# Two transformer-like layers on one core: the squares of two blocks folded to 64 columns before the norm matmuls, and one set of additions moved one tile earlier

## The chip, the cores and the metric

The kernel runs on one core of one Trainium2 chip. The metric is device time in microseconds (us) of the whole launch. The engines are TensorE (PE; its weight loads are shown apart as PEld), VectorE (DVE), ScalarE (ACT), GpSimd (POOL) and SyncE (SP, which here only starts DMAs).

## What is computed

Two attention layers and two gated layers, in turn, on 2048 tokens of 448 features. This is the reference, cut to its core:

```
def _A_ref(x, wqkv, wo):
    qkv = (x @ wqkv).reshape(B, S, 3, H, Dh), heads in front
    scores = einsum("bhqd,bhkd->bhqk", q, k) * (Dh ** -0.5)
    o = einsum("bhqk,bhkd->bhqd", softmax(scores), v)
    return o @ wo
def _B_ref(x, w_gate, w_up, w_down):
    return (sigmoid(x @ w_gate) * (x @ w_up)) @ w_down
x = A_x
x = x + _A_ref(_layernorm(x), A_wqkv, A_wo)
x = x + _B_ref(_layernorm(x), B_w_gate, B_w_up, B_w_down)
x = x + _A_ref(_layernorm(x), A_wqkv, A_wo)
x = x + _B_ref(_layernorm(x), B_w_gate, B_w_up, B_w_down)
```

## The kernel before

The tokens are worked on in four blocks of 512 (`NB` = 4, `W` = 512). Every fp32 operand is split into a high and a low fp16 part, so that a product is the sum of several fp16 matmuls. A layer has four stages: `project` (queries, keys, values), `attend`, `out_project`, and `gated`.

The change lies in `project` of the first layer, and there in `qk` (L834), which makes queries and keys of one block as seven tiles of 128 features by 512 tokens. For a tile:

- PE does 11 matmuls of 512 columns into one of four PSUM banks (L649).
- ACT copies the high part out of the bank (L883), DVE takes the low part (L884), and ACT squares the high part into `sq`, bf16, 128x512 (L886).
- DVE folds `sq`: it takes the larger of the first and the second half of its columns (L890), so that 256 are left. The loop there has two widths, 256 and 128, and stops at `few`, which is 256.
- SP starts the DMA of the tile to DRAM (L893).
- `norm_products` (L843) is put into the list `late`. It multiplies the folded `sq` by a table `ind` that sums over the features of each head, into PSUM (L845 for queries, L848 for keys). The largest such sum of a head bounds its scores, and keeps the exponentials in range: since the maximum over tokens is all that is wanted, folding by maximum only makes the bound a little looser.

`late` holds three tiles back: the norm matmul of tile i stands in PE's order behind the products of tile i+3. The last three tiles of a block are popped by `finish` (L899), which also reduces the 256 columns to one on DVE (L904, for queries and for keys). `finish` of block 2 is called within block 3, behind the products of its tiles 1 and 2; `finish` of block 3 is called in `guard_of_norms`, behind the first tile of values of block 2 (`vals`, 11 matmuls of 448 columns).

Beside each tile runs a list of other steps, `fill`: `fill[i]` is issued behind tile i. In blocks 2 and 3 of the first layer these are the splitting of the next block's operand (`b3.ready`: ACT L234, L239 and DVE L235, L240) and six steps `Measure.add` (L1313). Each of these sums the squares of a part of the weights of the later stages on DVE (L1318, a pass over up to 1792 columns with an accumulator read behind it, and a copy, L1322); the last, for gate and up, has one pass on DVE and one on ACT (L1325). All is issued in program order on each engine; no scheduler moves it.

```
for n in (W // 2, P):
    if n >= few:
        nc.vector.tensor_tensor(sq[:, 0:n], sq[:, 0:n], sq[:, n:2 * n], op=ALU.max)
```

The second layer makes queries and keys in another way (`qk_sums`), and folds its squares in two steps, of 2x128 and 2x64 columns (L961); its norm matmuls have 64 columns (L923), and its reductions 128 (L1101).

Of the kernel before, what the change touches and what calls it, by code (L numbers as in the profile page):

```python
# [19 lines left out]
P = 128  # L20
# [8 lines left out]
W = TB * P  # L29
# [48 lines left out]
ALONE = 3  # L78
CHUNK = D * NF // 7
SUMS_AT = ((("w", 3), 74), (("u", 0), 122), (("u", 6), 236))  # L80

N_SLOTS = 19
N_QUART = 12
# [44 lines left out]
def interleaved_layers(ctx: ExitStack, tc: tile.TileContext, x_in, wqkv, wo, w_gate, w_up,  # L128
# [31 lines left out]
    def bank(i, name):  # L160
        return psum(f"bank{i}", name, [P, 512])
# [479 lines left out]
    def by_features(pm, blk, wh, wl, some=range(11)):  # L641


        terms = [(w(kt), x[:, kt, :]) for kt in range(3)
                 for w, x in ((wh, blk.hi), (wh, blk.lo), (wl, blk.hi))]
        terms += [(w(3), blk.tail) for w in (wh, wl)]
        for i in some:
            w, x = terms[i]
            nc.tensor.matmul(pm, w, x, start=(i == 0), stop=(i == 10))  # L649
# [171 lines left out]
    def project(layer, wq, begun):  # L821
# [4 lines left out]
        def ones_of_values():  # L826
            for v in values:
                nc.gpsimd.memset(v[:, :, :, DH:VC], 0.0)
                nc.gpsimd.memset(v[:, :, :, DH:DH + 1], 1.0)
# [4 lines left out]
        def qk(b, blk, fill, before, ahead=()):  # L834
            pn = [bank(4 + 2 * (b % 2), "qnorm"), bank(5 + 2 * (b % 2), "knorm")]
            late = deque()
            few = W // 2

            def rows_of_heads(i):

                return ind[:, i:i + P // H, :].rearrange("p a h -> p (a h)")

            def norm_products(i, sq):  # L843
                if i <= 3:
                    nc.tensor.matmul(pn[0][:, 0:few], rows_of_heads(i), sq[:, 0:few],  # L845
                                     start=(i == 0), stop=(i == 3))
                if i >= 3:
                    nc.tensor.matmul(pn[1][:, 0:few], rows_of_heads(1 + i), sq[:, 0:few],  # L848
                                     start=(i == 3), stop=(i == 6))
                qrt.put(sq)  # L850

            def products(pm, i, some=range(11)):
                c = slice(i * P, (i + 1) * P)
                by_features(pm, blk, lambda kt: wq.qk[0][:, kt, c],
                            lambda kt: wq.qk[1][:, kt, c], some)

            begun = deque()
            if layer == 0 and b == 0:
                begun.extend(bank(i, "qkp") for i in range(2))
                for i, some in ((0, (0, 3, 1, 6, 2, 5, 8, 4)), (1, (0, 3, 6)), (0, (7,)),  # L860
                                (1, (1, 4, 7)), (0, (9, 10))):
                    products(begun[i], i, some)
            rest = {0: (), 1: (2, 5, 8, 9, 10), 4: (0, 3, 6, 1, 4, 7, 9, 2, 5, 8, 10)}

            for i in range(7):
                c = slice(i * P, (i + 1) * P)
                pm = begun.popleft() if begun else bank(evac[0] % 4, "qkp")
                evac[0] += 1
                if layer == 0 and b == 0:
                    products(pm, i, rest.get(i, range(11)))  # L870
                else:
                    products(pm, i)
                if layer == 0 and b == 0:
                    along[i]()
                if before and i in (1, 2):
                    before(i == 2)
                if len(late) == 3:
                    late.popleft()()
                hl = qrt.get("qkhl", [P, 2, W], F16)
                sq = qrt.get("sq", [P, W], BF16)  # L880
                if i < len(ahead) and ahead[i]:
                    ahead[i]()
                nc.scalar.activation(hl[:, 0, :], pm, AF.Copy, scale=PS)  # L883
                nc.vector.scalar_tensor_tensor(hl[:, 1, :], pm, PS, hl[:, 0, :], op0=ALU.mult,  # L884
                                               op1=ALU.subtract)
                nc.scalar.activation(sq, hl[:, 0, :], AF.Square)  # L886

                for n in (W // 2, P):
                    if n >= few:
                        nc.vector.tensor_tensor(sq[:, 0:n], sq[:, 0:n], sq[:, n:2 * n],  # L890
                                                op=ALU.max)
                n = slice(b * W, (b + 1) * W)
                nc.sync.dma_start(qk_scr[c, :, n], hl)  # L893
                qrt.put(hl)
                late.append(lambda i=i, sq=sq: norm_products(i, sq))
                if i < len(fill) and fill[i]:
                    fill[i]()

            def finish(whole=True):  # L899

                while len(late) > (0 if whole else 1):
                    late.popleft()()
                for i in range(2 if whole else 0):
                    nc.vector.tensor_reduce(peaks[:, i, b:b + 1], pn[i][0:H, 0:few], axis=AX.X,  # L904
                                            op=ALU.max)
            return finish
# [217 lines left out]
        def vals(b, blk, after, tiles=range(TB), at=None, begun=None, banks=None):  # L1124
            for j in tiles:
                if banks:
                    pv = bank(banks[j], "vp")
                else:
                    pv = begun or bank(evac[0] % 4 if at is None else at, "vp")
                    evac[0] += 1  # L1130
                values_product(pv, blk, j, range(2, 4) if begun else range(4))
                if j in after:
                    after[j]()
                v, pv = values[b][:, j, :, 0:DH], pv[:, 0:D].rearrange("p (h d) -> p h d", d=DH)
                if at is None:
                    nc.scalar.activation(v, pv, AF.Copy, scale=PS)
                else:
                    nc.vector.tensor_scalar(v, pv, PS, None, op0=ALU.mult)
            if tiles[-1] == TB - 1:
                blk.drop()  # L1140
# [22 lines left out]
        blks = begun + [Block(b, layer == 1, True) for b in range(len(begun), NB)]  # L1163
        idle = None
        sq = lambda b, *js: lambda: blks[b].squares(js)
        b1, b2, b3 = blks[1:]
# [22 lines left out]
        if layer == 0:  # L1189
            fin = qk(0, blks[0], fill, None, ahead)  # L1190
            vals(0, blks[0], along_values)
            fill = [b2.gather, b3.norm, sq(3, 0, 1), sq(3, 2, 3), idle,
                    lambda: b2.ready(0, 1), lambda: (b2.ready(2, 3), b3.store())]
            fin = qk(1, b1, fill, None)
            vals(1, b1, {0: b3.gather, 2: fin})
            add = tell.add
            fin = qk(2, b2, [idle, lambda: b3.ready(0, 1), lambda: b3.ready(2, 3), idle, add, add,
                             add], None)
            fin = qk(3, blks[3], [add, add, add], fin)
        else:  # L1200
            b2.clear()
            ones_of_values()
            b3.apart = True
            h2, h3, s3 = b2.half_steps(), b3.half_steps(), b3.squared()
            both = lambda *steps: lambda: [do() for do in steps]
            order = (3, 0, 1, 6)
            fin = qk_sums(0, blks[0], {0: b1.later + s3[0:1], 1: h2[0:1], 2: h2[1:2], 3: s3[1:2],
                                       4: h2[2:3], 5: [s3[2], s3[3], s3[6]]})
            vals(0, blks[0], {0: both(s3[4], s3[7]), 1: both(s3[5], s3[8], h2[3]),
                              2: both(fin, s3[9], b3.store, h2[4]),  # L1210
                              3: both(h2[5], b3.gather, b3.clear)}, banks=order)
            fin = qk_sums(1, b1, {0: h2[6:7], 1: h2[7:8], 3: h2[8:9], 4: h2[9:10]})
            vals(1, b1, {1: both(fin, h3[0]), 2: both(*h3[1:3]), 3: both(*h3[3:5])}, banks=order)
            fin = qk_sums(2, b2, {0: h3[5:6], 1: h3[6:7], 2: h3[7:8], 3: h3[8:9], 4: h3[9:10]},
                          None, True)
            fin = qk_sums(3, b3, {}, fin)
# [137 lines left out]
    class Prepare:  # L1354
# [3 lines left out]
        def __init__(self):  # L1358
# [9 lines left out]
            at, measured = 6, (6, 10, 16, 19, 22, 26)  # L1368
            for j, (behind, _) in enumerate(SUMS_AT):
                i = [what for _, what in order].index(behind)  # L1370
                order.insert(i + 1, (self.split, ("q", j)))
            for i, (do, what) in enumerate(order):
                if do == self.measure:
                    at = measured[i]
                then = order[i + 1][1] if i + 1 < len(order) else None
                self.steps.append((SUMS_AT[what[1]][1] if what[0] == "q" else at,
                                   lambda do=do, what=what, then=then:
# [940 lines left out]
```

## Time and profile before

| | before |
|---|---|
| three runs | 1869.34, 1869.38, 1869.78 us (median 1869.38) |
| the profiled execution | 1869.45 us, span 1867.7 us |
| PE busy (matmuls) | 1861.4 us, 24479 matmuls |
| DVE busy | 1462.4 us, 2933 instructions |
| ACT busy | 1404.2 us |
| POOL busy | 306.4 us |
| granted TensorE clock | 1.00 over the span |

Times in the trace are us from the start of the span. The stage of the change, blocks 2 and 3 of the first layer's queries and keys, lies at 66 to 104 us. In a timeline a row has the start, the busy time of the row (from its first start to its last end), engine, line, operation, what is written and read with its shape, the count, and in brackets how long the engine sat idle before and what released it. The ends of matmuls are modelled and overlap with the next; what a matmul costs is therefore read from the start of one to the start of the next. DVE's instructions overlap too, by some hundredths of a us.

### The profile page before, as it was taken

To read this page: it belongs to the slowest core of one execution; us is meant where nothing else is said; L and a number is where in the kernel's file an instruction comes from. 1 tells how busy PE (TensorE), PEld (TensorE's weight loads), DVE (VectorE), ACT (ScalarE), POOL (GpSimd) and SP (SyncE) were. 2 spreads that over 40 slices of the span, in tenths; PEclk is the share of its full clock that TensorE was granted. 3 is DMA by queue.
4 is the path that set the end of the run, shared out by engine and by line. 5 is a ranking of instruction groups with operands and counts; after the bars stand their busy time and mean duration, and the time that the engine had idled before them with its cause. 6 is when DMAs were issued, how large, how long until landed. Compare 5 with 4: busy or idle time off the path is not lost. (4 is left out here: it accounts for less than half of the span.)

```text
span 1867.7 us, 57157 instructions
## 1 busy us (share of the span) xinstructions
PE 1861.4 (100%) x24479; PEld 1416.1 (76%) x24479; DVE 1462.4 (78%) x2933; ACT 1404.2 (75%) x1865; POOL 306.4 (16%) x582
## 2 busy tenths in 40 slices
PE   9999999999999999999999999999999999999999
PEld 4455566656565899999987568888877668999999
DVE  7748898998997888788877477777777688887764
ACT  6569999999993655555567899999999746555541
POOL 3001123453412111212122000000000031121110
PEclk9999999999999999999999999999999999999999
DMA  7674454454433866757764322122120258677653
GB/s 265 182 214 130 131 160 128 125 156 113 136 129 86 288 211 229 244 204 257 243 187 109 88 52 52 27 53 52 30 50 14 79 165 264 210 249 239 235 201 144
DMA packets 114885, 286.24 MB, mean 153 GB/s; under 512 B 15134, under 2 KB 68878, under 8 KB 114496
## 3 DMA queue, kind: packets, MB, share of 16 engines
q0 software_dynamic: 35088, 174.86, 27.8%
q1 hardware_dynamic: 78384, 106.27, 20.3%
q8 instruction: 194, 3.18, 0.7%
q10 hardware_dynamic: 1152, 1.38, 0.3%
q14 instruction: 67, 0.55, 0.1%
HBM read 218.20 MB, written 54.29 MB: 146 GB/s over the span
## 5 line engine op out<-in xcount | busy, mean ns | idle before, releaser
L1574 ACT ACTIVATE prob_s<-sc 128x1536 f32<-128x1536 f32 (+1 forms) x657 | 888.1, 1484 | 5.9 <-PE sc L1559 3.0
L1609 PE MATMUL acc<-prob_s,val_s 128*32 128x256 f32 (+3 forms) x7708 | 587.2, 384 | 0.0
L1559 PE MATMUL sc<-qp_s 114*32 114x512 f16 x7868 | 571.3, 379 | 0.0
L1559 PEld LDWEIGHTS <-qp_s 114*32 114x32 f16 x8192 | 309.9, 96 | 168.8 <-issue 70.8
L1609 PEld LDWEIGHTS acc<-prob_s,val_s 128*32 128x32 f32 x7708 | 314.1, 110 | 100.3 <-issue 9.2
L1944 PE MATMUL dnp<-dn_s,hparts_s 128*128 128x224 f16 x2184 | 245.8, 259 | 0.0
L664 PEld LDWEIGHTS <-gue_s 128*128 128x128 f16 x2240 | 218.8, 98 | 24.5 <-PE op L1738 0.7
L1944 PEld LDWEIGHTS <-hparts_s 128*128 128x128 f16 x2184 | 210.2, 98 | 5.1
L664 PEld LDWEIGHTS <-gul_s 128*128 128x128 f16 x2016 | 197.0, 98 | 19.9
L664 PE MATMUL chain<-xwide_s,gue_s 128*128 128x256 f16 x1680 | 210.9, 273 | 0.0
L1589 DVE SCALAR_TENSOR_TENSOR power_q<-power_q,expo_q 128x512 f32<-128x512 f32 x243 | 168.2, 692 | 8.3
L664 PE MATMUL side<-xshort_s,gul_s 128*128 128x256 f16 x1344 | 165.0, 273 | 0.0
L2017 ACT COPY one_q<-chain 128x256 f32<-128x256 f32 x224 | 83.1, 372 | 105.4 <-PE chain L664 104.6
L2033 DVE TENSOR_TENSOR one_q<-side,one_q 128x512 f32<-128x512 f32 x112 | 74.3, 689 | 39.1 <-PE side L664 38.8
L1638 DVE STREAM_TRANSPOSE oturned_q<-acc 128x512 f32<-128x512 f32 x32 | 23.0, 717 | 98.4 <-PE acc L1609 98.2
L2044 ACT ACTIVATE one_q<-one_q 128x512 f32<-128x512 f32 x56 | 35.3, 630 | 79.8 <-DVE one_q L2033 79.8
L1609 PE MATMUL acc<-power_q,val_s 128*32 128x256 f32 (+3 forms) x300 | 94.2, 396 | 0.0
L1584 DVE TENSOR_SCALAR expo_q<-aside,base 128x512 f32<-128x512 f32 x81 | 60.6, 748 | 40.5 <-PE aside L1559 40.1
L587 POOL TENSOR_SCALAR rs<-mv 128x1 f32<-128x1 f32 x8 | 1.5, 191 | 505.8 <-DVE mv L585 505.8
L664 PE MATMUL chain<-xshort_s,gul_s 128*128 128x256 f16 x672 | 82.5, 273 | 0.0
L1902 DVE TENSOR_TENSOR hparts_s<-hsums_q,hparts_s 128x256 f16<-128x256 f32 (+1 forms) x152 | 71.3, 519 | 11.1 <-ACT hparts_s L1898 11.1
L664 PE MATMUL side<-xwide_s,gue_s 128*128 128x256 f16 x560 | 79.4, 273 | 0.0
(273 smaller groups left out, 2559.0 us busy)
## 6 DMA issues: line engine op xcount, KB each, us to landing
gue_s<-gu_early POOLq DMA_DIRECT2D x52, 960.0 KB, 5.3
gul_s<-gu_late POOLq DMA_DIRECT2D x52, 768.0 KB, 4.7
dn_s<-dn_parts POOLq DMA_DIRECT2D x42, 784.0 KB, 6.7
qp_s<-qk_scr SPq DMA_DIRECT2D x96, 224.0 KB
xt_scr<-xs_s SPq DMA_DIRECT2D x48, 224.0 KB
xraw_s<-xt_scr SPq DMA_DIRECT2D x12, 768.0 KB
qk_scr<-qkhl_q SPq DMA_DIRECT2D x28, 256.0 KB
qp_s<-qk_scr SPq DMA_DIRECT2D x64, 112.0 KB
```

What stands on the lines that cost most here:

```text
L664: nc.tensor.matmul(pm, a, x, start=(first and i == 0), stop=(i == len(terms) - 1), skip_group_check=True)
L1559: nc.tensor.matmul(ps[32 * j:32 * j + 32, :], hd.k[:, keys], hd.q[:, qb * W:(qb + 1) * W], start=True, stop=True, tile_position=(0, 32 * j))
L1574: nc.scalar.activation(prob[:, 0:n, :], ps[:, 0:n, :], AF.Exp, scale=exp_scale)
L1584: nc.vector.tensor_scalar(y, ps, base2[:, 0:1], -116.0, op0=ALU.mult, op1=ALU.max)
L1589: nc.vector.scalar_tensor_tensor(p, p, c[k], y, op0=ALU.add, op1=ALU.mult)
L1609: nc.tensor.matmul(acc[qb * VC:(qb + 1) * VC, s], v[:, kc % TB, h, :], probs[c * NB + qb][:, s], start=(kc == 0 and a == 0), stop=(kc == N ...
L1638: nc.vector.transpose(turned.rearrange("p b c -> p (b c)"), acc)
L1902: nc.vector.tensor_tensor(to[:, :, 1], a, to[:, :, 0], op=ALU.subtract)
L1944: nc.tensor.matmul(pm, a[:, x, t], w[:, p, y], start=(begin and n == 0 and (j == 0 or alone)), stop=(n == 2), skip_group_check=True)
L2017: nc.scalar.copy(to, pm)
L2033: nc.vector.tensor_tensor(one[m], side[m], one[m], op=ALU.add)
L2044: nc.scalar.activation(out, v, AF.Sigmoid, scale=gate_scale)
```

## The change

`few` becomes 64 for blocks 2 and 3 of the first layer, and the loop has a third width; so each of their 14 tiles is folded three times (256, 128 and 64 columns are left) instead of once, the 16 norm matmuls have 64 columns instead of 256, and the four reductions of `finish` read 64 columns instead of 256. `Measure.add` is issued behind tiles 3 to 6 of block 2 and 0 and 1 of block 3, where it was issued behind tiles 4 to 6 and 0 to 2. Blocks 0 and 1, and the second layer, are as before. In the new file all lines from L84 on are two higher.

```
+FOLDED_FROM = 2
...
-            few = W // 2
+            few = 64 if b >= FOLDED_FROM else W // 2
...
-                for n in (W // 2, P):
+                for n in (W // 2, P, 64):
                     if n >= few:
                         nc.vector.tensor_tensor(sq[:, 0:n], sq[:, 0:n], sq[:, n:2 * n],
                                                 op=ALU.max)
...
-            fin = qk(2, b2, [idle, lambda: b3.ready(0, 1), lambda: b3.ready(2, 3), idle, add, add,
+            fin = qk(2, b2, [idle, lambda: b3.ready(0, 1), lambda: b3.ready(2, 3), add, add, add,
                              add], None)
-            fin = qk(3, blks[3], [add, add, add], fin)
+            fin = qk(3, blks[3], [add, add], fin)
```

On DVE, tiles 3, 4 and 5 of block 2 before the change (L884 is the low part of a tile, L890 the fold of its squares, L1318 and L1322 an addition of `Measure`):

```order
L884 SCALAR_TENSOR_TENSOR qkhl_q_885<-qkp_872,qkhl_q_885 128x512
L890 TENSOR_TENSOR sq_q_886<-sq_q_886 128x256
L884 SCALAR_TENSOR_TENSOR qkhl_q_905<-qkp_892,qkhl_q_905 128x512
L890 TENSOR_TENSOR sq_q_906<-sq_q_906 128x256
L1318 ISA junk_s_912,part_237<-raw_s_458,sums 128x1568
L1318 ISA part_237 128x1
L1322 COPY sums<-part_237 128x1
L884 SCALAR_TENSOR_TENSOR qkhl_q_928<-qkp_915,qkhl_q_928 128x512
```

The same place with the change, from tile 3 on:

```order
L886 SCALAR_TENSOR_TENSOR qkhl_q_891<-qkp_878,qkhl_q_891 128x512
L892 TENSOR_TENSOR sq_q_892<-sq_q_892 128x256
L892 TENSOR_TENSOR sq_q_892<-sq_q_892 128x128
L892 TENSOR_TENSOR sq_q_892<-sq_q_892 128x64
L1320 ISA junk_s_900,part_237<-raw_s_458,sums 128x1568
L1320 ISA part_237 128x1
L1324 COPY sums<-part_237 128x1
L886 SCALAR_TENSOR_TENSOR qkhl_q_916<-qkp_903,qkhl_q_916 128x512
L892 TENSOR_TENSOR sq_q_917<-sq_q_917 128x256
L892 TENSOR_TENSOR sq_q_917<-sq_q_917 128x128
L892 TENSOR_TENSOR sq_q_917<-sq_q_917 128x64
L1320 ISA junk_s_925,part_237<-raw_s_460,sums 128x1792
```

Each tile has two folds more, each reading what the one before it wrote, and the first addition has come in front of tile 4, the second in front of tile 5; so it goes on to the end of block 2.

On PE, the first norm matmul of block 2, between the products of tile 3 and tile 4, before and with the change:

```order
L845 LDWEIGHTS ind
L845 MATMUL qnorm_804<-sq_q_819,ind 128x256
L649 LDWEIGHTS wqk_s_110
```

```order
L847 LDWEIGHTS ind
L847 MATMUL qnorm_804<-sq_q_819,ind 128x64
L651 LDWEIGHTS wqk_s_110
```

Its place is the same, its width a quarter; the other 15 change in the same way. SP and POOL issue what they issued, in the same order; on ACT one pass of `Measure` (L1325) comes one tile earlier.

## Rows read from the trace of the kernel before

**Rows 1.** Busy time in one stretch: PE, PEld, DVE, ACT, POOL, clock, DMA share, GB/s

```profile
84.00:92.00 8.00, 8.00 (x40) 3.74 (x39) 7.93 (x13) 4.09 (x8) 0.00 (x0) 1.00 0.23 78
```

**Rows 2.** Waits between engines, 68 to 104 us: total, times, longest

```profile
DVE qkhl_q L884 <- ACT qkhl_q L883: 7.2, 3, 4.2
```

**Rows 3.** Timeline of DVE, blocks 2 and 3 of the first layer

```profile
76.61 1.29 DVE L235 TENSOR_TENSOR xhl_s<-xraw_s,xhl_s 128x512 f16<-128x512 f32 x2 [3.75 <-ACT xhl_s L234]
...
78.42 0.28 DVE L890 TENSOR_TENSOR sq_q<-sq_q 128x256 bf16<-128x256 bf16 x1
78.79 0.69 DVE L235 TENSOR_TENSOR xhl_s<-xraw_s,xhl_s 128x512 f16<-128x512 f32 x1
...
80.84 0.28 DVE L890 TENSOR_TENSOR sq_q<-sq_q 128x256 bf16<-128x256 bf16 x1
81.04 0.69 DVE L884 SCALAR_TENSOR_TENSOR qkhl_q<-qkp,qkhl_q 128x512 f16<-128x512 f32 x1
...
83.80 0.68 DVE L884 SCALAR_TENSOR_TENSOR qkhl_q<-qkp,qkhl_q 128x512 f16<-128x512 f32 x1
84.40 0.28 DVE L890 TENSOR_TENSOR sq_q<-sq_q 128x256 bf16<-128x256 bf16 x1
84.60 2.08 DVE L1318 CUSTOM_DVE_ANT_0 junk_s<-raw_s,sums 128x1792 bf16<-128x1792 f32 x1
...
86.80 0.69 DVE L884 SCALAR_TENSOR_TENSOR qkhl_q<-qkp,qkhl_q 128x512 f16<-128x512 f32 x1
...
95.21 0.40 DVE L904 TENSOR_REDUCE peaks<-knorm 16x1 f32<-16x256 f32 x1
95.54 0.67 DVE L884 SCALAR_TENSOR_TENSOR qkhl_q<-qkp,qkhl_q 128x512 f16<-128x512 f32 x1
...
99.78 0.29 DVE L890 TENSOR_TENSOR sq_q<-sq_q 128x256 bf16<-128x256 bf16 x1
101.60 0.69 DVE L884 SCALAR_TENSOR_TENSOR qkhl_q<-qkp,qkhl_q 128x512 f16<-128x512 f32 x1 [1.53 <-ACT qkhl_q L883]
```

**Rows 4.** Timeline of PE, blocks 2 and 3 of the first layer

```profile
75.82 0.27 PE L845 MATMUL qnorm<-sq_q,ind 128*128 128x256 bf16 x1
75.93 2.54 PE L649 MATMUL qkp<-xhl_s,wqk_s 128*128 128x512 f16 x11
78.31 0.27 PE L845 MATMUL qnorm<-sq_q,ind 128*128 128x256 bf16 x1
...
88.24 0.38 PE L848 MATMUL knorm<-sq_q,ind 128*128 128x256 bf16 x2
...
100.77 0.27 PE L845 MATMUL qnorm<-sq_q,ind 128*128 128x256 bf16 x1
...
103.07 0.49 PE L848 MATMUL knorm<-sq_q,ind 128*128 128x256 bf16 x3
103.39 0.35 PE L674 MATMUL vp<-wv_s,xhl_s 128*128 128x448 f16 x1
```

**Rows 5.** Timeline of DVE, second layer: folds of `qk_sums`, and its reductions

```profile
955.32 0.55 DVE L961 TENSOR_TENSOR sq_q<-sq_q 128x256 bf16<-128x256 bf16 x2 [0.32 <-ACT sq_q L957]
955.83 0.69 DVE L945 SCALAR_TENSOR_TENSOR qkhl_q<-two_q,qkhl_q 128x512 f16<-128x512 f32 x1
...
961.43 0.55 DVE L961 TENSOR_TENSOR sq_q<-sq_q 128x256 bf16<-128x256 bf16 x2
...
961.75 0.23 DVE L961 TENSOR_TENSOR sq_q<-sq_q 128x128 bf16<-128x128 bf16 x1
961.89 0.68 DVE L945 SCALAR_TENSOR_TENSOR qkhl_q<-two_q,qkhl_q 128x512 f16<-128x512 f32 x1
...
1026.63 0.47 DVE L1101 TENSOR_REDUCE peaks<-norms 16x1 f32<-16x128 f32 x2 [0.33 <-PE norms L923]
```

**Rows 6.** Timeline of PE, second layer: norm matmuls of 64 columns

```profile
1025.94 0.65 PE L923 MATMUL norms<-sq_q,ind 128*128 128x64 bf16 x14
1026.42 0.73 PE L1118 MATMUL vp<-wv_s,xshort_s 128*128 128x448 f16 x3
```

## The prediction

> **What bounds the kernel now.** Over the whole span PE is busy, and in the stretch from 84 to 92 us it is busy for all 8.00 us at a granted clock of 1.00, the level of 2.4 GHz [rows 1]. So far PE sets the time, and a shorter norm matmul would shorten it. The same row has DVE at 7.93 of 8.00 us; a second engine is as full. The table of waits says how full: from 68 to 104 us DVE waits three times for the high part of a tile, 7.2 us in all, 4.2 at the longest [rows 2]. The last of these is the 1.53 us up to 101.60; the other two belong to tiles 0 and 1 of block 2, and another idle time of 3.75 us ends at 76.61 [rows 3]. Between 76.61 and 99.98, that is the last fold of a full stretch at 99.78 plus its 0.20 us, DVE has no idle at all. PE doesn't feel it, since norms are taken three tiles late. The reader is to see in rows 3 and 4 how far DVE is behind: the low part of tile 5 of block 2 begins at 83.80, its norm matmul is the second of the pair at 88.24, 3.4 us after the fold's end at 84.68; the last fold of block 3 ends near 102.6 (101.60 + 0.69 + 0.29) and its norm matmul is the third of those at 103.07, 0.5 us later. The slack shrinks from 3.4 to 0.5 us. The question is whether the added folds are cheaper than that.
>
> **PE's part.** The norm matmul of 256 columns costs 75.93 - 75.82 = 0.11 us from start to start [rows 4]. Fourteen of 64 columns in the second layer, each with its weight load, take 1026.42 - 1025.94 = 0.48 us, 0.034 each [rows 6]. Sixteen are shortened: 16 x 0.075 = 1.2 us. This is worth something only while PE waits for nobody.
>
> **DVE's part, for one tile.** One fold of 256 columns now costs 81.04 - 80.84 = 0.20 us before the next, independent instruction starts [rows 3]. In the new chain each fold reads what the one before wrote. The second layer has such a pair: the fold of 2x128 columns starts at 961.43, the one of 2x64 that reads it at 961.75, so 0.32 us, and the next instruction at 961.89, 0.14 later [rows 5]. A dependent start thus comes about 0.04 us behind the end (0.28 busy, then 0.32), where an independent one comes before it. For the new chain: 0.32 from the first to the second fold; the second, of 128 columns, is busy 0.23, so 0.27 to the third; the third has 64 columns, and as the independent interval falls from 0.20 to 0.14 between 256 and 128 columns, I take 0.11 (an estimate from these rows). The sum is 0.70, against 0.20: **0.50 us more for each tile.** The bounds: 0.25, if the dependent starts cost no more than independent ones (0.14 + 0.11); 0.63, if the instruction behind the third fold also waits for its end (0.20 busy and 0.04 in place of 0.11). I take 0.50, because the pair in rows 5 is the same operation, type and count of columns, and it was measured in a stretch just as full.
>
> What one rule would say: the Trainium skill, "VectorE: DVE Perf Modes", section "The DRAIN you can't avoid", holds that a chain with a semaphore after each operation took as long as one without, so the wait costs nothing extra. The trace does not agree: 0.32 us dependent, 0.20 independent for the same 256 columns. By the rule the tile would pay 0.25 us; its time is the first rival below.
>
> **DVE's part, summed.** Tiles 0 and 1 of block 2 lie before 76.61, where DVE is idle anyway: nothing. From 76.61 on there are tiles 2 to 6 of block 2 and 0 to 5 of block 3 before the last tile's turn: 11 x 0.50 = 5.5 us. Against it stand the two reductions of block 2 in this stretch: 0.33 us each now (95.21 to 95.54) [rows 3]; of 128 columns the pair in the second layer is busy 0.47, which with the same overlap of 0.07 is 0.20 each [rows 5]; the same slope gives 0.14 for 64, so 0.4 us saved for two. And 0.17 us is filled that DVE now waits for ACT (78.42 + 0.20 to 78.79). Sum: 5.5 - 0.4 - 0.2 = 4.9 us. DVE is ready for the last tile of block 3 at 99.98 + 4.9 = 104.9 instead of 99.98; it began that tile at 101.60, so it loses 3.3 us there, and the 1.53 us of idle are gone.
>
> **The end of the stretch.** From the low part at 104.9: 0.6 to the first fold, 0.32 and 0.27 to the third, 0.2 busy, 0.05 until PE starts (an estimate, as DVE's own dependent start takes 0.04): 106.35. Behind the norm matmul, PE goes on with values at 106.4; before, at 103.39 [rows 4]. That is **3.0 us later.** Is PE itself later than that? It isn't: its waits come earlier, in the norms. Tile 5 of block 2 now stands behind two additions of `Measure` instead of one, and three longer folds: 83.80 + 2.20 + 1.5 - 0.2 = 87.3, folded by 87.3 + 0.6 + 0.8 = 88.7; PE comes to its norm at 87.9 (88.24 less five norms' gain) and waits 0.8 us. By the same steps it waits about 1.1 us each for tile 6 of block 2 and tile 0 of block 3, and 0.2 and 0.4 for the next two. The products of the last tile ended at 100.77 [rows 4]; with 3.6 us of waits and the gain of 11 norms, 0.8, they end at 103.6. ACT then hands the tile to DVE 0.83 us later (101.60 - 100.77, when DVE waited for nothing else), at 104.4, before DVE is free. Two short norms and the 11 matmuls of values (103.07 - 100.99 = 2.1) bring PE to 105.7, where it waits the last 0.6 us. So all of PE's 1.2 us and 3 us more go into waits for the folds; PE's own price does not enter the end.
>
> **The additions one tile sooner** cost and save nothing in this sum: they stay within the stretch in which DVE has no idle, so the work in front of the last tile is the same 4.9 us more. They only bring PE's waits forward. ACT's pass moves with them, and ACT is far from full (4.09 of 8.00 us) [rows 1]. DMAs: as many, from the same places; a tile's store starts behind its low part, so the last ones are up to 3.3 us later, as is everything behind them. **Behind the stretch** PE runs through values and scores without idle; what DVE, POOL and SP do for the bounds hangs on PE's norms and moves along. Nothing there gives the 3.0 us back.
>
> The profiled execution took 1869.45 us, 0.07 more than the median of 1869.38. 1869.45 + 3.0 - 0.07 = **1872.4 us**, 0.16% slower; less than 0.2% (3.7 us) is about what a measurement of this kernel can tell from no change.
>
> **Rivals.** *The chain is no dearer than independent folds.* 0.25 us per tile: 11 x 0.25 - 0.6 = 2.1, so DVE is free at 102.1, and the tile comes from ACT at about that time. By the steps above PE waits some 0.7 and 0.9 us, at the norms of tile 6 of block 2 and tile 0 of block 3, and gains 1.2: about 0.4 us slower, 1869.8. For it: the rule above, whose copies were not of this kind. Against: rows 5, in both pairs. Chance 0.10.
>
> *PE stays the bound.* If the folds hid in the slack, the 1.2 us of PE would be the result: 1868.2. For it: PE is what has no idle now. Against: the slack ends at 0.5 us, and DVE has 1.5 us of idle for 4.9 us of work; it decides only below some 0.2 us per tile. Chance 0.03.
>
> *DVE is held at the end of each chain* (the slower side). If the low part or the addition behind the third fold starts only after its end, a tile costs 0.63: 11 x 0.63 - 0.6 = 6.3, and the end lies 4.4 us later: 1873.8. It passes 0.2% from 0.56 us per tile on. For it: one pair in rows 5, whose next instruction came 0.19 us behind the second fold's start (955.32 + 0.55 - 0.23 = 955.64, then 955.83). Against: that one may have waited for its own input, and the pair at 961.75 did not. Chance 0.13.
>
> **How the numbers follow.** The forecast has 0.74, with a range of its own of 0.44 to 0.56 us per tile: 1871.8 to 1873.1. The range takes in the third rival's lower part and reaches down to the first rival's time: 1869.8 to 1873.6; below it lies PE's rival, above it the rest of the third. Faster by over 0.2% would be below 1865.6: none of the cases gives it, 0.01. Slower by over 0.2% is above 1873.1: the third rival and a piece of the forecast's upper end, 0.18. Within it: 0.81.
>
> **What would show it.** In the timeline of DVE the three folds start 0.32 and 0.27 us apart, and the next instruction 0.11 behind the third; DVE has no idle from 76.6 to about 105. The table of waits has PE (or its weight loads of `ind`) waiting for `sq`, some 4 us in five or six waits from 88 us on; the last norm matmul starts at 106.35. The norm matmuls cost 0.03 us. The prediction is wrong if PE has no wait there, if a chain takes under 0.55 or over 0.8 us, or if the first scores, now behind values, don't move by the same 3 us as the last norm.

## The result and the profile after

The changed kernel takes **1872.74 us** (median of 22 runs, 1871.93 to 1874.62) against 1869.58 us for the kernel before (median of 22 runs beside them, 1869.11 to 1871.08): 3.16 us more, a ratio of 1.0017 with a 95% interval of 1.0011 to 1.0024. The ratio lies inside the 0.2% that counted as no change, near its slow end; the interval reaches a little beyond it.

| | before | after |
|---|---|---|
| median | 1869.58 us | 1872.74 us |
| the profiled execution | 1869.45 us, span 1867.7 us | 1874.13 us, span 1872.4 us |
| PE busy | 1861.4 us | 1861.5 us |
| DVE busy | 1462.4 us, 2933 instructions | 1467.1 us, 2961 instructions |
| granted TensorE clock | 1.00 | 1.00 |

The profiled execution after is 1.39 us slower than its median; the reason is found below. PE's busy time is the same and the span 4.7 us longer: what was added on PE is idle time. In the new file a line number from L84 on is two higher.

First the timeline of DVE after, the same stretch as [rows 3] (start, busy time, engine, line, operation, what is written and read, count, idle time before and its releaser):

```profile
77.74 1.29 DVE L237 TENSOR_TENSOR xhl_s<-xraw_s,xhl_s 128x512 f16<-128x512 f32 x2 [4.26 <-ACT xhl_s L236]
78.95 0.68 DVE L886 SCALAR_TENSOR_TENSOR qkhl_q<-qkp,qkhl_q 128x512 f16<-128x512 f32 x1
79.55 0.77 DVE L892 TENSOR_TENSOR sq_q<-sq_q 128x256 bf16<-128x256 bf16 x3
80.24 0.69 DVE L237 TENSOR_TENSOR xhl_s<-xraw_s,xhl_s 128x512 f16<-128x512 f32 x1
...
89.00 0.77 DVE L892 TENSOR_TENSOR sq_q<-sq_q 128x256 bf16<-128x256 bf16 x3
89.69 2.08 DVE L1320 CUSTOM_DVE_ANT_0 junk_s<-raw_s,sums 128x1792 bf16<-128x1792 f32 x1
...
100.50 0.20 DVE L906 TENSOR_REDUCE peaks<-qnorm 16x1 f32<-16x64 f32 x1
100.62 0.20 DVE L906 TENSOR_REDUCE peaks<-knorm 16x1 f32<-16x64 f32 x1
100.76 0.67 DVE L886 SCALAR_TENSOR_TENSOR qkhl_q<-qkp,qkhl_q 128x512 f16<-128x512 f32 x1
...
105.88 0.68 DVE L886 SCALAR_TENSOR_TENSOR qkhl_q<-qkp,qkhl_q 128x512 f16<-128x512 f32 x1
106.48 0.77 DVE L892 TENSOR_TENSOR sq_q<-sq_q 128x256 bf16<-128x256 bf16 x3
```

The three folds of a tile hold DVE from 79.55 to 80.24, 0.69 us, where one fold held it 0.20 us [rows 3]. Within the row of three they start at 79.55, 79.87 and 80.13, so 0.32 and 0.26 us apart, and the next instruction starts 0.11 us behind the third. The two reductions start 0.12 to 0.14 us apart. From 77.74 to the last tile's low part at 105.88 no row of this engine has an idle time, and that tile, for which DVE waited 1.53 us before [rows 3], now waits for DVE. The work from the first row to that low part is 28.14 us; before it was 99.98 - 76.61 = 23.37 us. So 4.77 us were added.

The timeline of PE after, as [rows 4]:

```profile
75.96 0.19 PE L847 MATMUL qnorm<-sq_q,ind 128*128 128x64 bf16 x1
75.99 2.54 PE L651 MATMUL qkp<-xhl_s,wqk_s 128*128 128x512 f16 x11
...
89.83 0.20 PE L850 MATMUL knorm<-sq_q,ind 128*128 128x64 bf16 x1 [1.60 <-DVE sq_q L892]
...
93.33 0.20 PE L850 MATMUL knorm<-sq_q,ind 128*128 128x64 bf16 x1 [0.92 <-DVE sq_q L892]
...
96.82 0.20 PE L847 MATMUL qnorm<-sq_q,ind 128*128 128x64 bf16 x1 [0.92 <-DVE sq_q L892]
...
102.17 0.20 PE L847 MATMUL qnorm<-sq_q,ind 128*128 128x64 bf16 x1 [0.21 <-DVE sq_q L892]
...
107.30 0.20 PE L850 MATMUL knorm<-sq_q,ind 128*128 128x64 bf16 x1 [0.36 <-DVE sq_q L892]
107.34 0.35 PE L676 MATMUL vp<-wv_s,xhl_s 128*128 128x448 f16 x1
```

A norm matmul now costs 0.03 us (75.96 to 75.99) instead of 0.11. Five of them wait for the folds, together 4.0 us, and PE goes on with values at 107.34 instead of 103.39.

The busy time of 84 to 92 us after, as [rows 1] (PE, PEld, DVE, ACT, POOL, clock, DMA share, GB/s), shows the same from afar. PE has fallen from 8.00 to 6.40 of 8.00 us, and it is still granted the full 2.4 GHz:

```profile
84.00:92.00 8.00, 6.40 (x32) 2.77 (x30) 7.76 (x18) 4.36 (x8) 0.00 (x0) 1.00 0.24 80
```

The waits after, 68 to 110 us (who for whom, total, times, longest), as [rows 2]:

```profile
DVE qkhl_q L886 <- ACT qkhl_q L885: 4.7, 2, 3.7
ACT xhl_s L236 <- DMA xraw_s<-xt_scr: 4.4, 1, 4.4
...
PE knorm L850 <- DVE sq_q L892: 2.9, 3, 1.6
```

DVE has two waits for a tile's high part where it had three, and PE's waits for the folds are new. The wait for the rows of block 3 (`xraw_s`) will matter below.

### The profile page after: what moved, and what is told of

It reads as the page before. It is cut to its first block, busy times and chain, and to the rows that moved or that the text cites. A ratio compares the mean times of both kernels' runs of the same rounds, so it can differ in the third digit from the quotient of the medians.

```text
span 1872.4 us, 57182 instructions
## 1 busy us (share of the span) xinstructions
PE 1861.5 (99%) x24479; PEld 1364.4 (73%) x24479; DVE 1467.1 (78%) x2961; ACT 1404.0 (75%) x1865; POOL 307.8 (16%) x582
## 5 line engine op out<-in xcount | busy, mean ns | idle before, releaser
L1611 PE MATMUL acc<-prob_s,val_s 128*32 128x256 f32 (+3 forms) x7708 | 575.5, 383 | 0.0
L1561 PE MATMUL sc<-qp_s 114*32 114x512 f16 x7868 | 559.0, 379 | 0.0
L1561 PEld LDWEIGHTS <-qp_s 114*32 114x32 f16 x8192 | 285.4, 96 | 191.8 <-issue 83.5
L1611 PEld LDWEIGHTS acc<-prob_s,val_s 128*32 128x32 f32 x7708 | 287.0, 110 | 127.5 <-issue 10.8
```

What stands on the lines that cost most here:

```text
L1561: nc.tensor.matmul(ps[32 * j:32 * j + 32, :], hd.k[:, keys], hd.q[:, qb * W:(qb + 1) * W], start=True, stop=True, tile_position=(0, 32 * j))
L1611: nc.tensor.matmul(acc[qb * VC:(qb + 1) * VC, s], v[:, kc % TB, h, :], probs[c * NB + qb][:, s], start=(kc == 0 and a == 0), stop=(kc == N ...
```

## The experiments

The theory was that the longer folds alone make the time: the stretch is set by DVE from the splitting of block 3's operand on, and the additions' new place costs nothing. The rivals were that the additions' place does it, that the dependent starts of the folds cost nothing, and that PE would gain if DVE had room. Each kernel was timed in five rounds beside the kernel before, which took 1869.36 (e1 to e4), 1869.39 (e5 to e8) and 1869.30 us (e9 to e11).

### One part alone: the folds, the additions

e1_fold_only takes the change and puts the additions back:

```
-            fin = qk(2, b2, [idle, lambda: b3.ready(0, 1), lambda: b3.ready(2, 3), add, add, add,
+            fin = qk(2, b2, [idle, lambda: b3.ready(0, 1), lambda: b3.ready(2, 3), idle, add, add,
                              add], None)
-            fin = qk(3, blks[3], [add, add], fin)
+            fin = qk(3, blks[3], [add, add, add], fin)
```

> The folds to 64 columns as in the change, the additions of Measure where they were before. Theory (DVE without idle from the landing of block 3's rows to the last tile; only its total work sets the end): the additions lie within that stretch either way, so the time is that of the change, 3.0 us above before (about 1872.6), give or take 0.5. Rival (the additions one tile sooner are what hurts, or what helps): below 1871 if they hurt, above 1874 if they help.

Measured: 1871.93 us, 2.57 more than before (ratio 1.0014, 1.0005 to 1.0023). The folds alone make most of the change.

e5_shift_only takes the kernel before and has only the additions one tile sooner (the two `fin =` lines above, the other way round).

> No folds beyond 256 columns; the additions of Measure one tile sooner as in the change. Theory: DVE's work in the stretch is the same, and its slack covers the order: 0.0 against before, give or take 0.3; where block 3's rows land a us late, up to 0.8 more. Rival (the additions' new place is a cost of its own, seen as the difference of the change and e1_fold_only): 0.6 us or more above before in the median.

Measured: 1869.91 us, 0.52 more (1.0002, 0.9993 to 1.0011). That is more than was expected, and its interval alone doesn't exclude nothing. It was repeated as e10_shift_again:

> e5_shift_only once more, beside e9_slots_only. Theory and rival: 0.4 to 0.6 us above before again, if it is a property of the kernel; 0.0 if it was the state of that chip.

Measured: 1870.07 us, 0.77 more (1.0005, 0.9996 to 1.0014). The 2.57 of the folds and this 0.5 to 0.8 add up to the change's 3.16. But PE has no wait in the stage in e5, so the cost had to be found elsewhere; see "Where the additions cost".

e8_change_again is the change a second time:

> The change itself, beside the others on one chip. Theory: 2.5 to 3.2 us above before, as e1_fold_only; its executions spread by some 2 us, as they follow the landing of block 3's rows, where those of before spread by less. Rival: 0.6 us more than e1_fold_only on one chip too, as the earlier additions would cost that.

Measured: 1872.25 us, 2.86 more (1.0014, 1.0005 to 1.0023).

### Half of the fold

e6_fold_128 is the change with two folds for each tile instead of three, so that its norm matmuls have 128 columns:

```
-            few = 64 if b >= FOLDED_FROM else W // 2
+            few = P if b >= FOLDED_FROM else W // 2
```

> The change with folds to 128 columns only (two folds, norm matmuls of 128 columns). Theory: a tile costs 0.46 us instead of 0.70, which frees 11 x 0.24 = 2.6 us of the stretch; the time lies 0.5 to 1.5 us above before (about 1870.4), between before and the change. Rival (the width of the norm matmuls, not DVE, sets the time): at or below before.

Measured: 1870.31 us, 0.92 more (1.0004, 0.9995 to 1.0013). The number is the one expected, but the theory gives only a part of it: in the profiled execution the stage is 0.28 us longer than before, and 0.74 us are lost far behind it (intervals A and C of the table below).

### Room on DVE

e2_early_adds moves four of the six additions of the kernel before into idle time of DVE before block 3's operand comes: two behind values of block 1, one each behind tiles 0 and 1 of block 2. e3_early_adds_fold does so with the folds to 64 columns.

```
-            vals(1, b1, {0: b3.gather, 2: fin})
             add = tell.add
-            fin = qk(2, b2, [idle, lambda: b3.ready(0, 1), lambda: b3.ready(2, 3), idle, add, add,
+            vals(1, b1, {0: b3.gather, 2: fin, 3: lambda: (add(), add())})
+            fin = qk(2, b2, [add, lambda: (add(), b3.ready(0, 1)), lambda: b3.ready(2, 3), idle, add,
                              add], None)
-            fin = qk(3, blks[3], [add, add, add], fin)
+            fin = qk(3, blks[3], [], fin)
```

> No folds beyond 256 columns; the first four additions of Measure moved into DVE's idle time in front of the stretch (two behind the values of block 1, one behind each of tiles 0 and 1 of block 2), the other two behind tiles 4 and 5 of block 2. Theory: PE waits for nobody before, so 8.6 us less DVE work in the stretch gains nothing: 0.0, give or take 0.3. Rival (DVE's fullness already costs PE something before the change): 0.5 us or more faster.

> The folds to 64 columns, with the additions as in e2_early_adds. Theory: the folds' 5 us fit into the 8.6 us that DVE is freed of, PE waits for no fold, and its own saving of 16 x 0.075 us is left: 1.1 to 1.2 us faster than before (about 1868.4), with a spread as small as that of before. Rival (the chain of folds is late for its norm by its own length, not by DVE's queue): still 1 us or more slower than before.

Measured: e2 1869.43 us, 0.07 more (0.9999, 0.999 to 1.0008); e3 **1868.03 us**, 1.33 less (0.9993, 0.9984 to 1.0002). Repeated as e11_early_fold_again:

> e3_early_adds_fold once more, to have its gain from two sets of executions. Theory: 1.1 to 1.4 us faster than before again. Rival (its gain was that of other buffers in attention, not of the shorter norm matmuls): half of that or less.

Measured: 1868.11 us, 1.19 less (0.9993, 0.9984 to 1.0003). The timeline of PE in e3:

```profile
101.95 0.39 PE L850 MATMUL knorm<-sq_q,ind 128*128 128x64 bf16 x3
102.18 0.35 PE L676 MATMUL vp<-wv_s,xhl_s 128*128 128x448 f16 x1
```

and of DVE in e3:

```profile
100.64 0.69 DVE L886 SCALAR_TENSOR_TENSOR qkhl_q<-qkp,qkhl_q 128x512 f16<-128x512 f32 x1 [0.96 <-ACT qkhl_q L885]
101.30 0.78 DVE L892 TENSOR_TENSOR sq_q<-sq_q 128x256 bf16<-128x256 bf16 x3
```

No norm is listed with a wait, DVE is idle again before the last tile, and values go on at 102.18 instead of 103.39 [rows 4]. Only the very last norm comes a little late: the three rows take 102.18 - 101.95 = 0.23 us, where three short norms cost 0.09, since the last fold ends at 102.08 (101.30 + 0.78). So the shorter norms are worth about the 1.2 us that the sum for PE gave, once DVE has room. Each interval still includes 1, but both runs lie 1.2 to 1.3 us below the kernel before and 4.1 to 4.7 below the change and its repeat. It is the fastest version seen.

### The price of the dependent starts

In e4_independent the second and third fold of a tile read and write another buffer of zeros, so they wait for nothing. The norms take the first 64 of 256 columns, so three quarters of the tokens are left out of the bound.

```
+                        v = {W // 2: sq, P: other[0], 64: other[0][:, W // 2:]}[n] if few == 64 else sq
-                        nc.vector.tensor_tensor(sq[:, 0:n], sq[:, 0:n], sq[:, n:2 * n],
+                        nc.vector.tensor_tensor(v[:, 0:n], v[:, 0:n], v[:, n:2 * n],
                                                 op=ALU.max)
```

> The change, but the second and third fold of each tile work on another tile of memory, so that they wait for nothing; the norms then take only the first 64 of the 256 columns, three quarters of the tokens are left out of the bound. Theory (a fold that reads the one before starts 0.32 and 0.27 us behind it, an independent one 0.20 and 0.14): a tile costs 0.45 us instead of 0.70, 11 tiles 2.7 us less, and the time is 0.3 to 0.8 us above before (about 1870.1). Rival (waiting inside a chain costs nothing extra, only the number of operations counts): as the change, 3 us above before.

Measured: 1869.10 us, 0.26 less (0.9999, 0.999 to 1.0008). The timeline of DVE in e4, one tile:

```profile
79.97 0.28 DVE L894 TENSOR_TENSOR sq_q<-sq_q 128x256 bf16<-128x256 bf16 x1
80.16 0.32 DVE L894 TENSOR_TENSOR other_q<-other_q 128x128 bf16<-128x128 bf16 x2
80.40 1.84 DVE L1325 CUSTOM_DVE_ANT_0 junk_s<-raw_s,sums 128x1568 bf16<-128x1568 f32 x1
```

The three folds take 80.40 - 79.97 = 0.43 us when they are independent, against 0.69. The dependences cost 0.26 us for each tile, 2.9 us over the 11 tiles: about as much as the whole loss of e1 (2.57 us). The Trainium skill, "VectorE: DVE Perf Modes", section "The DRAIN you can't avoid", holds that a semaphore after each operation of a chain costs nothing extra; for folds this small these rows say otherwise. The time came out 0.6 us below the lowest expected. The expectation had not counted two things: a norm here waits for the first fold only, and in the profiled execution block 3's operand came 0.76 us earlier against PE than in that of before (0.03 us behind the first norm instead of 0.79; A less B in the table below). What each of them gave is not measured. So e4 shows the folds' price by its rows, not by its time.

### The start of DVE's stretch

e7_ready_later splits block 3's operand one tile later in the order, so that the low part of a tile of block 2 stands before the wait for it:

```
-            fin = qk(2, b2, [idle, lambda: b3.ready(0, 1), lambda: b3.ready(2, 3), add, add, add,
-                             add], None)
+            fin = qk(2, b2, [idle, idle, lambda: b3.ready(0, 1), lambda: (b3.ready(2, 3), add()),
+                             add, add, add], None)
```

> The change, with the splitting of block 3's operand issued one tile later (behind tiles 2 and 3 of block 2), so that the low part and the three folds of tile 2 lie in DVE's idle time in front of the landing of block 3's rows. Theory: 1.3 us of DVE work leave the stretch that begins at the landing, so the time lies about 1.3 us below the change, 1.8 above before (about 1871.2). Rival (the end is set by the chain of the last tiles alone, not by when the stretch begins): as the change.

Measured: 1870.60 us, 1.21 more than before (1.0007, 0.9998 to 1.0016), and 1.65 less than the change beside it. The timeline of DVE in e7:

```profile
75.47 0.69 DVE L886 SCALAR_TENSOR_TENSOR qkhl_q<-qkp,qkhl_q 128x512 f16<-128x512 f32 x1 [0.93 <-ACT qkhl_q L885]
...
77.17 1.29 DVE L237 TENSOR_TENSOR xhl_s<-xraw_s,xhl_s 128x512 f16<-128x512 f32 x2 [0.26 <-ACT xhl_s L236]
```

A tile's work, about 1.3 us (0.6 for the low part and 0.69 for the folds), now lies in DVE's idle time before the operand. From the operand to values it is 28.32 us instead of 29.60: 1.28 less, on DVE's path as the theory wants. Attention is 0.6 us shorter too (C in the table below), for a reason of its own; that is more than the 0.37 us left of the 1.65, and how the rest comes about is not shown.

### Three intervals of every run

All of this shows in three intervals, each from two rows of a run's timelines. A: from PE's first norm of block 2 (75.82 before, [rows 4]) to the values behind the last norm (103.39). B: from DVE's first splitting of block 3's operand (76.61, [rows 3]) to the same values. C: from those values to the first row of DVE behind the attention of the 16th head. The last column is the median against the kernel before.

| | A | B | C | median |
|---|---|---|---|---|
| before | 27.57 | 26.78 | 460.12 | |
| the change, profiled | 31.38 | 29.60 | 460.82 | +3.16 |
| e8 the change again | 30.14 | 29.60 | 460.78 | +2.86 |
| e1 folds only | 30.04 | 29.60 | 460.18 | +2.57 |
| e7 splitting later | 28.48 | 28.32 | 460.17 | +1.21 |
| e6 folds to 128 | 27.85 | 27.56 | 460.86 | +0.92 |
| e5 additions only | 27.57 | 26.86 | 460.81 | +0.52 |
| e10 the same again | 27.57 | 27.20 | 460.80 | +0.77 |
| e9 buffers only | 27.57 | 27.17 | 460.77 | +0.64 |
| e2 early additions | 27.57 | 26.92 | 460.14 | +0.07 |
| e4 independent | 26.81 | 26.78 | 460.16 | -0.26 |
| e3 early additions, folds | 26.43 | 25.10 | 460.24 | -1.33 |
| e11 the same again | 26.43 | 25.10 | 460.18 | -1.19 |

Where a tile is folded once (before, e2, e5, e9, e10), A is 27.57 to the hundredth while B varies: PE sets the end. Where it is folded three times and the additions stay in the stretch (the change, e8, e1), B is 29.60 to the hundredth while A varies: DVE sets it, counted from the moment that block 3's rows have come. In e3 and e11 both are constant, since there the splitting begins behind DVE's early additions and not behind the rows; that PE sets the end again is read there from A, 1.14 us below 27.57 with no listed wait. C is as before in both, so their gain does not come from attention.

That DVE sets the end explains most of why the profiled execution was slow. In e8, the same kernel, the end of the stage is, on PE:

```profile
105.82 0.20 PE L850 MATMUL knorm<-sq_q,ind 128*128 128x64 bf16 x1 [0.36 <-DVE sq_q L892]
105.86 0.35 PE L676 MATMUL vp<-wv_s,xhl_s 128*128 128x448 f16 x1
```

and the start of DVE's stretch is:

```profile
76.26 1.29 DVE L237 TENSOR_TENSOR xhl_s<-xraw_s,xhl_s 128x512 f16<-128x512 f32 x2 [3.02 <-ACT xhl_s L236]
```

In e8 the splitting begins 0.54 us after PE's first norm (75.72), in the first profile 1.78 us after it (77.74 against 75.96); ACT waited 3.2 us for the rows there and 4.4 here. The last norm is later by 1.48 us, as the splitting is.

### Where the additions cost

Column C has two values, 460.12 to 460.24 and 460.77 to 460.86. Kernels with the second lose some 0.65 us that neither A nor B shows. The loss is in attention, far behind the changed lines. The rows that C is read from, before:

```profile
563.51 0.72 DVE L1638 STREAM_TRANSPOSE oturned_q<-acc 128x512 f32<-128x512 f32 x1 [3.00 <-PE acc L1609]
```

so 563.51 - 103.39 = 460.12, and in e9, described next:

```profile
103.34 0.35 PE L674 MATMUL vp<-wv_s,xhl_s 128*128 128x448 f16 x1
...
564.11 0.72 DVE L1640 STREAM_TRANSPOSE oturned_q<-acc 128x512 f32<-128x512 f32 x1 [3.02 <-PE acc L1611]
```

To see whether the instructions' order does it or the buffers that follow from it (the addition on ACT takes a buffer from a pool that the squares use), e9_slots_only keeps the order of the kernel before and takes that one buffer a tile sooner:

```
+        def reserve(self):
+            self.junk = qrt.get("junk", [P, CHUNK], BF16)
+            qrt.put(self.junk)
...
-                junk = qrt.get("junk", [P, n], BF16)
-                nc.scalar.activation(junk, t[:, n:2 * n], AF.Square, accum_out=sums[:, 5:6])
-                qrt.put(junk)
+                nc.scalar.activation(self.junk, t[:, n:2 * n], AF.Square, accum_out=sums[:, 5:6])
...
-            fin = qk(3, blks[3], [add, add, add], fin)
+            fin = qk(3, blks[3], [add, lambda: (add(), tell.reserve()), add], fin)
```

> The instructions of before in their old order; only the quarter-size buffers are handed out as in e5_shift_only and the change (one buffer is taken a tile sooner), so that 915 later requests get another buffer. It tells apart where the 0.5 us of e5_shift_only come from. Theory: they are not DVE's (its profile has no wait of PE in the stage), but lie in attention, where its heads took 0.45 us longer in all, and follow the buffers: 0.4 to 0.5 us above before here too. Rival (they come from the additions' order in the stage, in executions that were not profiled): 0.0 against before, give or take 0.2.

Measured: 1869.94 us, 0.64 more (1.0004, 0.9995 to 1.0013), with C at 460.77. So the loss comes without any instruction moved: handing out the quarter-size buffers as e5 does is enough to make it. The first 0.22 us are lost in the first head. The timeline of PE before, there:

```profile
136.22 0.83 PE L1609 MATMUL acc<-prob_s,val_s 128*32 128x384 f32 x8
136.87 0.83 PE L1559 MATMUL sc<-qp_s 114*32 114x512 f16 x12
```

and in e9:

```profile
136.17 0.83 PE L1611 MATMUL acc<-prob_s,val_s 128*32 128x384 f32 x8
136.96 0.83 PE L1561 MATMUL sc<-qp_s 114*32 114x512 f16 x12
```

The same step takes 0.65 us before and 0.79 in e9, and two smaller losses follow within 3 us. The waits of 134 to 142 us in e9 name the score's weight load, and no releaser:

```profile
PEld L1561 <- issue: 0.9, 4, 0.4
```

Before, the longest is 0.2 us:

```profile
PEld L1559 <- issue: 0.7, 4, 0.2
```

ACT's timeline shows where it begins. ACT takes the exponentials of the scores in passes of 1536 columns, and nearly every pass starts before the end of the one in front of it. Before:

```profile
132.53 2.87 ACT L1574 ACTIVATE prob_s<-sc 128x1536 f32<-128x1536 f32 x2
135.22 1.52 ACT L1574 ACTIVATE prob_s<-sc 128x1536 f32<-128x1536 f32 x1
```

and in e9:

```profile
132.47 2.88 ACT L1576 ACTIVATE prob_s<-sc 128x1536 f32<-128x1536 f32 x2
135.46 1.45 ACT L1576 ACTIVATE prob_s<-sc 128x1536 f32<-128x1536 f32 x1
```

Before, the third pass starts 0.18 us ahead of the second one's end (135.40); in e9 it starts 0.11 us behind it (135.35), and the scores at 136.96 start 0.05 us behind that pass's end (136.91). In the first layer's attention each trace has 330 such pairs of passes. In all thirteen traces one pass starts behind the end of the pass in front, by 0.33 us. In the six with the second value of C three more do, always the same three, by 0.10 to 0.12, under 0.02 and 0.05 to 0.08 us; in the seven others none. Why these passes start late, and what the buffers have to do with it, is open. That the additions stand one tile sooner isn't enough for it either: e7 and e4, whose additions stand as in the change, have the first value of C.

## Why the prediction was right, and where it was not

The forecast of 1872.4 us was 0.34 below the median of 1872.74, and the range of 1869.8 to 1873.6 held it. Its mechanism is the one found, but not all of the 3.16 us comes from it.

- **The added folds**, 0.50 us a tile: right. The chain takes 0.69 us (0.70 forecast) in place of 0.20. The two bounds that were left are excluded: 0.43 for three independent folds was measured by itself (e4), and nothing is held behind the third fold, whose successor starts at 0.69. The first rival's time was not right: it gave 0.4 us slower for independent folds, and e4, whose norms wait for the first fold only, came out 0.26 us faster.
- **The sum on DVE**, 4.9 us: 4.77 measured. The reductions, taken at 0.14, start 0.12 to 0.14 apart. That DVE had no idle at all from 76.61 to 99.98 is not quite so; the sum itself fills the 0.17 us that rows 3 show before 78.79.
- **The end of the stretch**, 3.0 us later: the forecast had 106.4 - 76.61 = 29.8 us from the operand to values, and it is 29.60. With the operand 0.79 us behind PE's first norm, as in the profile of before, that is 29.60 + 0.79 - 27.57 = 2.8 us later. The folds alone cost 2.57 in e1. The term was some 0.2 to 0.4 too large.
- **PE's waits**: five, at the norms named. Forecast were 0.8, 1.1, 1.1, smaller ones and 0.6 at the last; measured 1.60, 0.92, 0.92, 0.21 and 0.36. The first is longer since block 3's rows came 1.0 us later against PE in that execution; in e8, where they came 1.24 us sooner, it is 0.43. The step took the landing of one execution for fixed: it did not see that DVE, once it sets the end, hands every delay of that DMA on.
- **PE's gain**, 1.2 us only if PE waits for nobody: right both ways. It is nothing in the change, and e3, with room on DVE, has it: A is 1.14 us shorter. Sixteen norms at 0.08 (0.11 less 0.03) would be 1.3; the 0.14 us by which the last norm comes late are missing.
- **The additions one tile sooner** "cost and save nothing": this step failed. In the stretch it holds: A is 27.57 in e5, and B is the same with and without the shift. But the shift has the buffers behind it handed out otherwise, and attention takes some 0.65 us longer, as it does in e9 with no instruction moved. The prediction had said of what lies behind the stretch that nothing there gives the 3.0 us back; that it could add to them was not asked.
- **The first scores** were to move with the last norm, and do: 120.46 instead of 116.51 in the profiled execution, 3.95, as much as values (107.34 - 103.39).

So the total was near in part by luck, as two errors offset each other: folds at 3.0 instead of 2.6, and 0.65 us of attention at nothing.

## What to carry to other kernels

Saving time on the engine that is busy all the time is worth nothing if the work moves to a second engine that is as busy in that stretch; look for idle time of the second engine first, and move other work there (e3), and then the saving comes in full. A chain of small operations on one buffer is to be priced by dependent pairs in the trace, not by the interval of independent ones: here 0.69 against 0.43 us for three. When two rows of different engines are a constant interval apart over several executions, that pair shows what sets the time, and the interval that stopped being constant shows what no longer does; it needs executions in which the start of one of the two moves, as here with the landing of a DMA.

## What was not expected of the hardware

Two executions of one kernel differed by 1.82 us (1874.13 and 1872.31, the profiled ones of the change and of e8), of which 1.24 us are the landing of one DMA's rows against PE (1.78 and 0.54 us); before, PE's slack on that operand took this up. And the choice of buffers alone, with all instructions in place (e9), moved attention by 0.65 us, beginning with a pass of ACT that starts 0.11 us behind the end of the one in front, instead of 0.18 us ahead of it. The granted clock stayed at 1.00 in 84 to 92 us, though PE was busy for only 6.40 of 8.00 us and idle for up to 1.60 us at a time.
